# Two attention and GLU layers on one core: two weight pairs under way at a time, normalising and masking also on GpSimd, and another planned order

## The chip, the core and the metric

The kernel runs on one core of one Trainium2 chip. A core has five engines that run their own instruction streams side by side: TensorE (PE in the profile, its weight loads PEld) multiplies, VectorE (DVE) and ScalarE (ACT) work element by element and copy results out of PSUM, GpSimd (POOL) works element by element on SBUF alone, and SyncE (SP) issues most of the DMAs. Engines wait for each other through semaphores. The metric is the time of one execution on the device in microseconds (us). The time before is 389.96 us, the median of three runs (389.87 to 390.82).

## What is computed

A block A (sliding, dilated attention) and a block B (gated product) follow each other twice, each on the layer norm of x and each added to x. The sequence is 2048 rows of 448 columns; attention has 16 heads of 28 columns, and each row looks at itself and at 7 earlier rows, 2 apart. All is bfloat16.

```python
def _A_ref(x, wqkv, wo):
    q, k, v = qkv[0], qkv[1], qkv[2]            # x @ wqkv, 16 heads of 28
    idx = pos[:, None] - off[None, :]           # off = 0, 2, .., 14
    logits = jnp.einsum("bhsd,bhswd->bhsw", q, kg) * scale   # kg = k at idx
    logits = jnp.where(mask[None, None, :, :], logits, -1e9) # mask = idx >= 0
    attn = _softmax(logits, axis=-1)
    o = jnp.einsum("bhsw,bhswd->bhsd", attn, vg)
    return o @ wo

def _B_ref(x, w_gate, w_up, w_down):
    return ((x @ w_gate) * (x @ w_up)) @ w_down  # 448 -> 1792 -> 448

x = x + _A_ref(_layernorm(x), A_wqkv, A_wo)
x = x + _B_ref(_layernorm(x), B_w_gate, B_w_up, B_w_down)
x = x + _A_ref(_layernorm(x), A_wqkv, A_wo)
x = x + _B_ref(_layernorm(x), B_w_gate, B_w_up, B_w_down)
```

## The kernel before

x lies in SBUF as 16 blocks of 128 rows (x_sb). The four stages are numbered 0 (A), 1 (B), 2 (A), 3 (B); each is cut into chunks of rows, A0 and both B into 256, 512, 512, 512, 256 and A2 into four of 512. The list SEQ gives the chunks' rough sequence, so that work of a B chunk runs between the parts of an A chunk. The names below have the form name(stage, chunk or block or query block, ...), as the code's keys do.

**Layer norm and transposes.** ln_chunk makes the statistics of each block on DVE (bn, mv), the reciprocal deviation on ACT (lnv, rstd), and the normalised rows on DVE (xn, into one of five buffers xn_sb). For stage 0 PE transposes them (Tps, line 802; line 798 for the first two), and ACT or DVE copies them to xnTa (T). In the other stages the DMA engine transposes, issued by SP (line 791).

**Attention.** qk_chunk multiplies with WQK (line 535, key Kps/Qps), and ACT or DVE copies K and Q to qk (line 898). v_group makes V for a pair of query blocks. attn_front masks Q into two halves, Qz (line 1009: two instructions on DVE, one buffer for all groups), which zero the columns of the heads that are not meant; a burst of 64 small matmuls makes the scores S (line 1021), ACT takes the exponential (line 1030) and DVE applies the sliding mask (line 1037). attn_back makes another burst, AV (line 1055), copies the sums to O_sb, and norm divides. y_blocks multiplies with wo_g. The last heads' V (vt) is carried through DRAM: SP issues seven small DMAs a chunk (vt<-qk, line 907) and transposing loads (line 918).

**The B block.** b_chunk makes gate and up for each 128 of 1792 columns, two products side by side in the upper and lower 64 rows of PE (line 535); ACT copies the gate (g_sb, line 1146), DVE multiplies (hT, line 1149), and a second product with WD follows, added to x by DVE (line 1110).

**Bursts.** A burst's small matmuls use up instructions fast. Where a wide product is at hand, the planner puts some of its pairs into the burst as strips of 32 columns (line 538): 8 strips for a pair, 16 or 24 in a burst.

**Weights.** plain_dma (line 627) puts a DMA on SP's queue. WGU (gate and up) is loaded in two halves of columns of three pieces each (KPARTS), and every piece is a pair of DMAs, one for gate and one for up; WD follows in four pieces. The loop at line 726 makes each pair wait for the pair before it, through `gate`; the first pair waits for wo_g, and wo_g for x's third group of blocks (line 724). The pieces of one half share a semaphore, and a mode number tells the groups on it apart.

**What sets the order.** Nothing is ordered by hand. Each piece of work is handed to a planner (Sched) with the engines that may do it, an estimated duration for each, what it depends on, and a priority: the chunk's, plus PR for its kind, JP for its chunk and XP for single pieces. schedule runs a clock over these estimates; whenever an engine is free it takes the ready piece with the lowest number, and where two engines may do it, whichever comes first. HOLD_A, HOLD_BA and HOLD_BB say how long bursts may be held back to stand together, JOIN how many bursts may be joined, A_CAP and B_CAP how many PSUM banks each kind may hold. run_pe also estimates when a block of PE's instructions has been fetched, by fixed durations LINE_H, LINE_W and LINE_T for three phases of the run. emit then writes the instructions of each engine in this order, with semaphore waits: each engine runs them strictly in sequence, and so does SP's DMA queue.

## Time and profile before

| | |
|---|---|
| median of the runs | 389.96 us |
| profiled execution, its own time | 391.56 us |
| its span, first to last instruction | 389.6 us |
| PE busy | 380.8 us, 98% |
| DVE busy | 287.0 us, 74% |
| ACT busy | 209.0 us, 54% |
| POOL busy | 7.8 us, 2% |
| mean granted clock of TensorE | 0.996 |
| SP's and the other engines' plain DMAs (q1) | 54372 packets, 21.08 MB |
| instruction fetches (q8) | 52 packets, 0.85 MB |

The profiled execution is one execution, and the page and the trace tell of it alone. "Busy" of PE counts matmuls from their start to a modelled end, so that pipelined ones overlap. "issue" in the chain of work is time in which an engine waited for nothing that the profile shows. Line 535 is a helper that records every paired product, so one has to go by the tiles: xnTa,WQK is Q and K, WV,xnTa is V, wo_g,oT the attention's output, xnTb,WGU gate and up, WD,hT the second product of B.

### The profile page before, as it was taken

The page shows a single profiled execution, that of the slowest core. Times are in us where ns is not written, and L with a number is a line of the kernel's source. Part 1 is how long each engine was busy: PE and PEld are TensorE (multiplying, and loading weights), DVE is VectorE, ACT ScalarE, POOL GpSimd, SP SyncE. Part 2 cuts the span into 40 slices and gives each one's busy share as a digit, 9 for nine tenths or more (in the row PEclk, how much of TensorE's full clock was granted, in tenths as well). Part 3 has the DMA queues.
Part 4 walks back from the last instruction along what each step waited for, and adds up shares of the span by engine and source line. Part 5 has one row for each costly group of instructions (what it writes and reads, how often), then busy time and mean ns, then how long its engine had stood idle before and what let it go on. Part 6 is the DMA issues. An engine that isn't in the chain of part 4 may idle for free.

```text
span 389.6 us, 14816 instructions
## 1 busy us (share of the span) xinstructions
PE 380.8 (98%) x6565; PEld 214.7 (55%) x6565; DVE 287.0 (74%) x638; ACT 209.0 (54%) x393; POOL 7.8 (2%) x37
## 2 busy tenths in 40 slices
PE   8989989899999999999999999999999999999997
PEld 3646558455555544454766557654555444544584
DVE  6998989599968975399656997575967994376343
ACT  4887865397455775246454455565634842263140
POOL 6010000000000000000000000000000000000000
PEclk9989999999999999999999999999999999999999
DMA  8543574710711313004113132310133042100201
GB/s 276 161 106 76 137 101 124 122 23 9 87 25 34 47 39 56 10 6 86 21 22 50 30 63 37 75 32 2 27 54 96 3 47 52 48 2 3 60 14 49
DMA packets 54867, 22.53 MB, mean 58 GB/s; under 512 B 44996, under 2 KB 54804, under 8 KB 54804
## 3 DMA queue, kind: packets, MB, share of 16 engines
q1 hardware_dynamic: 54372, 21.08, 27.4%
q8 instruction: 52, 0.85, 0.9%
q10 hardware_dynamic: 432, 0.52, 0.5%
q14 instruction: 11, 0.09, 0.1%
HBM read 8.54 MB, written 2.71 MB: 29 GB/s over the span
## 4 chain that ended last, share of the span: by engine, by line
PE 93%; ACT 3%; DMA 1%; issue 1%; DVE 1%; SPq 0%; ACTq 0%
PE ps L535 82%; PE ps L538 3%; PE ps L1055 2%; PE ps L1021 2%; PE ps L697 2%; ACT E_sb L1030 1%; PE ps L1161 1%; DMA WD<-in_B_w_down_dram 1%; ACT xnTa L812 1%; ACT qk L898 1%; ACT g_sb L1146 0%; ACT xnTa L809 0%; DVE x_sb L1110 0%; PE ps L802 0%; DVE hT L1149 0%
## 5 line engine op out<-in xcount | busy, mean ns | idle before, releaser
L535 PE MATMUL ps<-xnTb,WGU 64*128 64x512 bf16 (+1 forms) x1908 | 174.4, 332 | 0.2
L535 PEld LDWEIGHTS ps<-xnTb,WGU 64*128 64x128 bf16 x1908 | 92.6, 94 | 67.8 <-issue 1.1
L1146 ACT ACTIVATE g_sb<-ps 128x512 bf16<-128x512 f32 (+1 forms) x140 | 71.1, 511 | 87.8 <-PE ps L535 71.7
L1149 DVE TENSOR_TENSOR hT<-g_sb,ps 128x512 bf16<-128x512 bf16 (+1 forms) x140 | 79.6, 576 | 43.1 <-ACT g_sb L1146 40.7
L535 PE MATMUL ps<-WD,hT 64*128 64x448 bf16 x778 | 78.6, 349 | 1.5 <-DMA WD<-in_B_w_down_dram 1.4
L535 PEld LDWEIGHTS ps<-WD,hT 64*128 64x128 bf16 x778 | 36.9, 94 | 36.0 <-issue 1.7
L535 PE MATMUL ps<-xnTa,WQK 64*128 64x512 bf16 (+1 forms) x492 | 55.2, 360 | 0.5 <-ACT E_sb L1030 0.3
L1110 DVE TENSOR_TENSOR x_sb<-x_sb,ps 128x448 bf16<-128x448 bf16 x62 | 36.4, 615 | 23.3 <-PE ps L535 23.3
L1030 ACT ACTIVATE E_sb<-ps,shift_sb 128x1024 bf16<-128x1024 f32 (+1 forms) x36 | 36.8, 1073 | 24.5 <-PE ps L1021 24.4
L767 DVE BATCH_NORM_STATS2 st<-x_sb 128x6 f32<-128x448 bf16 x64 | 37.7, 612 | 0.2
L788 DVE TENSOR_SCALAR xn_sb<-x_sb,mv,rstd 128x896 bf16<-128x896 bf16 (+1 forms) x64 | 34.7, 568 | 2.7 <-ACT rstd L772 2.5
L535 PEld LDWEIGHTS ps<-xnTa,WQK 64*128 64x128 bf16 x492 | 23.9, 96 | 22.2 <-issue 1.5
L898 ACT ACTIVATE qk<-ps 128x1024 bf16<-128x1024 f32 (+1 forms) x26 | 24.6, 956 | 11.3 <-PE ps L535 11.2
L535 PE MATMUL ps<-wo_g,oT 64*128 64x448 bf16 x256 | 29.1, 349 | 0.1
L1037 DVE TENSOR_TENSOR E_sb<-E_sb,MK 128x1024 bf16<-128x1024 bf16 (+1 forms) x36 | 23.6, 661 | 6.8 <-ACT E_sb L1030 6.5
L1081 ACT ACTIVATE R_sb<-R_sb 128x480 f32<-128x480 f32 (+1 forms) x34 | 20.5, 603 | 11.1 <-DVE R_sb L1080 10.6
L535 PE MATMUL ps<-WV,xnTa 64*128 64x336 bf16 (+3 forms) x248 | 23.1, 304 | 0.0
L1080 DVE STREAM_SHUFFLE R_sb<-O_sb 128x480 f32<-128x480 f32 (+1 forms) x34 | 23.1, 696 | 0.0
L1093 DVE TENSOR_TENSOR oT<-O_sb,R_sb 128x480 bf16<-128x480 f32 (+3 forms) x36 | 22.0, 624 | 0.8 <-ACT R_sb L1082 0.6
L1009 DVE TENSOR_SCALAR Qz<-qk,qmask 128x960 bf16<-128x960 bf16 (+1 forms) x36 | 14.7, 451 | 9.2 <-PE ps L1021 8.0
L1082 ACT ACTIVATE R_sb<-R_sb 128x480 f32<-128x480 f32 (+1 forms) x34 | 20.0, 600 | 0.3
L535 PEld LDWEIGHTS ps<-wo_g,oT 64*128 64x128 bf16 x256 | 12.4, 94 | 12.4 <-DVE oT L1093 0.9
(64 smaller groups left out, 231.6 us busy)
## 6 DMA issues: line engine op xcount, KB each, us to landing
out_dram<-x_sb SPq DMA_DIRECT2D x15, 112.0 KB, 1.7
x_sb<-in_A_x_dram SPq DMA_DIRECT2D x3, 448.0 KB, 6.0
WGU<-in_B_w_gate_dram SPq DMA_DIRECT2D x4, 224.0 KB, 3.6
WGU<-in_B_w_up_dram SPq DMA_DIRECT2D x4, 224.0 KB, 3.9
WD<-in_B_w_down_dram SPq DMA_DIRECT2D x2, 448.0 KB, 4.0
WGU<-in_B_w_gate_dram SPq DMA_DIRECT2D x2, 336.0 KB, 4.5
WGU<-in_B_w_up_dram SPq DMA_DIRECT2D x2, 336.0 KB, 6.3
vt<-qk SPq DMA_DIRECT2D x42, 16.0 KB
```

The source lines that it names most:

```text
L535: return lambda E: E.matmul(out(), lhs(), rhs(), start=start, stop=stop)
L767: sc.add("dve", one(lambda E, B=B: E.bn_stats(st6[:, B, :], x_sb[:, B, :]), ("bn", li, B)), 525.0, deps=[("x", li - 1, B)] + ([("xn", li - ...
L788: sc.add("dve", one(lambda E, B=B, dst=dst, src=src: E.tensor_scalar(dst, src, mv[:, B, 0:1], rstd[:, B:B + 1], ALU.subtract, ALU.mult), ( ...
L898: return E.activation(dst, src, ACT.Copy) if hasattr(E, "activation") else E.tensor_copy(dst, src)
L1030: return E.activation(E_sb[:, slot, 2 * hp:2 * hp + 2, 0:w], ps[:, b0:b0 + 2, 0:w], ACT.Exp, bias=shift_sb[:, 0:1], scale=SCALE)
L1037: return E.tensor_tensor(e, e, MK[:, kind, 0:nc].unsqueeze(1).unsqueeze(1).to_broadcast([128, 2, w // nc, nc]), ALU.min)
L1080: sc.add("dve", one(lambda E: E.stream_shuffle(R_sb[:, rs, 0:w], O_sb[:, os_, 0:w], [DH] * 32), ("Rs", li, qb)), dve_est(w) + 20.0, deps=[ ...
L1081: sc.add("act", one(lambda E: E.activation(R_sb[:, rs, 0:w], R_sb[:, rs, 0:w], ACT.Ln), ("Rl", li, qb)), act_est(w, False), deps=[("Rs", l ...
L1093: return E.tensor_tensor(oT[:, :, a % HALF:a % HALF + z - a], O[:, :, a - tok:z - tok], R_sb[:, rs, 0:w].rearrange("p (h n) -> p h n", h=4 ...
L1110: sc.add("dve", one(lambda E: E.tensor_tensor(x_sb[:, B, :], x_sb[:, B, :], ps[:, bk[w], 0:D], ALU.add), ("x", li, B)), dve_est(D), deps=[ ...
L1146: sc.add("act", one(lambda E, gs=gs, bk=bk: E.activation(g_sb[:, gs, 0:nt], ps[:, bk[0], 0:nt], ACT.Copy), ("G", li, j, fc)), act_est(nt), ...
L1149: sc.add("dve", one(lambda E, gs=gs, bk=bk, fc=fc: E.tensor_tensor(hT[:, fc, hs, 0:nt], g_sb[:, gs, 0:nt], ps[:, bk[1], 0:nt], ALU.mult), ...
```

## The change

Weights: the pieces of WGU, wo and WD now wait for the group two before, through a list `gates` of which each takes the last but one. The first pair waits for x's third group of blocks, the second for the fourth. wo_g is issued behind the first half of WGU and waits for that half's second pair; the second pair of the second half waits for wo_g together with the third pair of the first half; the ones for vt follow the first pair of the second half. Every piece has a semaphore of its own.

GpSimd: xn of stage 0 (but for the first chunk) and Qz of both A stages may be done by DVE or by GpSimd, whichever the planner finds free first. In the order that results, GpSimd does xn of blocks 2, 4, 8, 10, 14 and 15 and nine of the eighteen Qz.

Planner: the fixed durations of an instruction fetch give way to line_at, which takes into account the DMAs that were issued before and have not landed. JOIN, the HOLDs, ATT_P, B_CAP, HEAD_P, PR, JP and XP have other values. Together these give another order on every engine. The work is otherwise the same. The diff, without PR, JP and XP (lines of many numbers each):

```diff
-JOIN = 3
+JOIN = 2
-HEAD_P = (-7243.45, -6839.28, 6873.65, 2231.18, -2220.8)
-HOLD_A = 5940.0
-HOLD_BA = 13780.0
-HOLD_BB = 680.0
+HEAD_P = (-9131.1, -8282.44, 5502.77, 2529.68, -2872.96)
+HOLD_A = 4650.0
+HOLD_BA = 10410.0
+HOLD_BB = 1210.0
-ATT_P = 3.0
+ATT_P = 0.5
-B_CAP = 6
+B_CAP = 8
...
+    LINE_A = 1200.0
+    LINE_B = 1100.0
+    LINE_C = 2700.0
...
+    def line_at(self, at):
+        t = at + self.LINE_A
+        for issued, landed in self.moves:
+            if issued <= at + self.LINE_B:
+                t = max(t, landed - self.LINE_B)
+        return t + self.LINE_C
...
-            self.lines.append(at + (self.LINE_H if at < self.HEAD_T else self.LINE_W if at < self.HEAD_W else self.LINE_T))
+            self.lines.append(self.line_at(at))
...
-    plain_dma("sp", ones_dst, ones_src, ("vones",), "d_one", deps=["c_ones"] + [("wo", j) for j in range(4)], lat=4000.0, prio=-44.5)
-    for j in range(4):
-        dst = wo_g[32 * j:32 * j + DH, :, :]
-        src = A_wo.rearrange("(c j e) d -> j e c d", c=4, j=4, e=DH)[j]
-        plain_dma("sp", dst, src, ("wo", j), "d_wo", deps=["c_wo", ("x", -1, 11)], lat=3600.0, prio=-45)
-    gate = [("wo", j) for j in range(4)]
+    plain_dma("sp", ones_dst, ones_src, ("vones",), "d_one", deps=["c_ones", ("wu", 1, 0)], lat=6000.0, prio=-44)
+    gates = [[("x", -1, 11)], [("x", -1, 15)]]
     for n in range(2):
         f0, f1 = F // 2 * n, F // 2 * (n + 1)
         for i, (a, z) in enumerate(KPARTS):
             for w, lo, src in (("wg", 0, B_w_gate), ("wu", 64, B_w_up)):
-                plain_dma("sp", WGU[lo:lo + 64, a:z, f0:f1], src[64 * a:64 * z, f0:f1].rearrange("(k p) f -> p k f", p=64), (w, n, i), f"d_{w}{n}", deps=gate, lat=LOAD_L + 224 * (z - a) / RATE, prio=-44, mode=i)
-            gate = [("wg", n, i), ("wu", n, i)]
+                plain_dma("sp", WGU[lo:lo + 64, a:z, f0:f1], src[64 * a:64 * z, f0:f1].rearrange("(k p) f -> p k f", p=64), (w, n, i), f"d_{w}{n}{i}", deps=gates[-2], lat=1900.0 + 1000.0 * (z - a), prio=-44, est=650.0)
+            gates.append([("wg", n, i), ("wu", n, i)])
+        if n == 0:
+            for j in range(4):
+                dst = wo_g[32 * j:32 * j + DH, :, :]
+                src = A_wo.rearrange("(c j e) d -> j e c d", c=4, j=4, e=DH)[j]
+                plain_dma("sp", dst, src, ("wo", j), "d_wo", deps=["c_wo"] + gates[-2], lat=4000.0, prio=-44)
+            gates[-1] = gates[-1] + [("wo", j) for j in range(4)]
...
-        plain_dma("sp", WD[:, a:z, :], B_w_down[128 * a:128 * z, :].rearrange("(c p) e -> p c e", p=128), ("wd", n), f"d_wd{n // 2}", deps=gate, lat=LOAD_L + 112 * (z - a) / RATE, prio=-44, mode=n % 2)
-        gate = [("wd", n)]
+        plain_dma("sp", WD[:, a:z, :], B_w_down[128 * a:128 * z, :].rearrange("(c p) e -> p c e", p=128), ("wd", n), f"d_wd{n}", deps=gates[-2], lat=4200.0, prio=-44)
+        gates.append([("wd", n)])
...
-            sc.add("dve", one(lambda E, B=B, dst=dst, src=src: E.tensor_scalar(dst, src, mv[:, B, 0:1], rstd[:, B:B + 1], ALU.subtract, ALU.mult), ("xn", li, B)),
-                   325.0 if par == 0 else 540.0, deps=[("rstd", li, B), ("mv", li, B), ("x", li - 1, B), prev], prio=prio - 0.2)
+            sc.add(("dve", "pool") if li == 0 and j else "dve", one(lambda E, B=B, dst=dst, src=src: E.tensor_scalar(dst, src, mv[:, B, 0:1], rstd[:, B:B + 1], ALU.subtract, ALU.mult), ("xn", li, B)),
+                   {"dve": 325.0 if par == 0 else 540.0, "pool": 800.0}, deps=[("rstd", li, B), ("mv", li, B), ("x", li - 1, B), prev], prio=prio - 0.2)
...
-        sc.add("dve", [((lambda E, a=a: fz(E, a)), ("Qz", li, g) if a else None) for a in range(2)], 2 * (4 * (end - tok) * 0.33 + 62.0), deps=qdeps + [zprev, "c_qm"], prio=prio)
+        sc.add(("dve", "pool"), [((lambda E, a=a: fz(E, a)), ("Qz", li, g) if a else None) for a in range(2)], {"dve": 2 * (4 * (end - tok) * 0.33 + 62.0), "pool": 2 * (4 * (end - tok) * 1.25 + 100.0)}, deps=qdeps + [zprev, "c_qm"], prio=prio)
```

## The prediction

> **What bounds it.** I read the page first, then PE's busy time in stretches of 3.4 us, then the chain of work in the stretches that stood out, then the waits, the DMA queues and single rows for prices.
>
> ```profile
> PE 380.8 (98%) x6565; PEld 214.7 (55%) x6565; DVE 287.0 (74%) x638; ACT 209.0 (54%) x393; POOL 7.8 (2%) x37
> PEclk9989999999999999999999999999999999999999
> q8 instruction: 52, 0.85, 0.9%
> PE 93%; ACT 3%; DMA 1%; issue 1%; DVE 1%; SPq 0%; ACTq 0%
> ```
>
> PE is the bound: 93% of the chain. A new order can only take back the time in which PE stands or runs slowly, so I looked for that. The stretches (window, its length, busy of PE, PEld, DVE, ACT, POOL, granted clock, DMA share, GB/s):
>
> ```profile
> 19.81:23.22 3.41, 3.28 (x82) 1.54 (x74) 3.14 (x9) 2.95 (x10) 0.45 (x3) 1.00 0.19 47
> 23.22:26.64 3.42, 1.88 (x94) 1.41 (x96) 3.42 (x12) 3.42 (x6) 0.57 (x3) 1.00 0.34 96
> 26.64:30.05 3.41, 3.41 (x34) 2.11 (x30) 2.02 (x4) 2.30 (x4) 0.00 (x0) 0.50 0.83 186
> 47.12:50.53 3.41, 2.19 (x84) 1.29 (x82) 2.25 (x4) 3.17 (x6) 0.00 (x0) 1.00 0.59 88
> 67.60:71.01 3.41, 2.00 (x30) 1.32 (x30) 2.48 (x6) 1.83 (x6) 0.00 (x0) 1.00 0.88 217
> ```
>
> Four losses show. From 23.22 PE is busy 1.88 of 3.42 us while DVE and ACT are full (3.42 each): the layer norm and copies behind the transposes are late. The next stretch is granted half the clock (0.50), which costs 1.7 us. At 47 and 67 PE stands again. From 90 us on, PE is busy 10.00 of 10 us nearly everywhere. The chain, and the wait behind the last loss:
>
> ```profile
> 48.59 0.22 PE ps L1021 x16
> 48.81 1.22 issue
> 50.03 0.47 PE ps L1021 x26
> ...
> 66.43 3.96 DMA WD<-in_B_w_down_dram
> 70.48 1.50 PE ps L535 x14
> ```
>
> ```profile
> PE ps L535 <- DMA WD<-in_B_w_down_dram: 1.4, 1, 1.4
> ```
>
> At 66.43 the last quarter of WD is issued, four microseconds before PE needs it. At 48.81 PE waits in a burst of small matmuls for nothing that a semaphore tells. The DMA view of 44 to 47 us has only this for its queues:
>
> ```profile
> q1 hardware_dynamic: 471, 0.67, 95.1%
> ```
>
> In 47 to 50 one packet of the instruction queue appears. By the page that queue moved 52 packets, 0.85 MB, 16 KB each, for PE's 13,130 instructions (two a matmul): one block is 126 matmuls. I read the stand as a code block held behind the last weight pair, which filled the engines until 47.
>
> **The change, part by part.** The changed program has as many matmuls within 20 and the same products; its first 100 and last 25 of 391 PE groups follow nearly the old sequence.
>
> Weights. Before, one pair (gate and up piece) is under way at a time: issues at 16.4, 21.0, 25.7, 32.3, 37.1, 42.3, and WD from 52.1 to 66.4, landing at 70.4. Now the first pair waits for x block group 2 (11.5 us, where wo was issued) and two are under way; wo goes behind the first half of gate and up, 4 issues of about 0.4 us on SP. Bytes: 3.2 MB WGU, 1.6 MB WD, 0.4 MB wo. At the 224 GB/s of the 44 to 47 view they need 23 us, so the earliest end is 35 us; with nothing gained by the overlap it is 65. I take a cycle of 2.9 us a pair of two pieces (between 2.05 of data and 4.65 now), 4.0 for three: 19.6 + 2.5 for wo + 8 for WD, an end at about 42. First uses are at 55 (WGU) and 68 (WD), so WD's wait goes: 1.4. Next late is hT of the first B chunk, whose last row ends at 68.4, before the wait's start at 69.1; its chain has 0.4 us steps, so at most 0.6 of the gain is lost to it. I take -1.3, bounds -1.4 and -0.8.
>
> SP. Every weight issue now stands ahead of the first vt<-qk (before, six stood behind it). SP is past its last weight wait at about 38 by the same cycles; vt<-qk was issued at 38.92. If it were late, the vt loads are wanted at 80 (30 us of cover), the first xnTb transposes (47.6 before) at 55.6: 8 us of cover. The ones load now follows WGU's second half and is wanted only by those vt loads. Nothing.
>
> Head. Six of the sixteen xn and nine of the eighteen Qz go to GpSimd, and four more xnTa copies go from ACT to DVE. DVE's own work ahead of xn of the last-but-one block, summed by rows (statistics 0.612 + 0.170, xn 0.403, xnTa 0.416, Qz 0.345 or 0.464, casts 1.22, masks 0.45), is 25.8 us before (the trace has it at 25.9) and 20.4 after. So PE paces this stage. After 9.78 it has, up to its thirteenth narrow transpose, 28 pairs of 256 columns at 0.112, 28 of 512 at 0.216 (94.08 to 97.10 is 14 pairs), V 2.0 and 13 transposes at 0.2: 13.8 us, so 23.6; the copies that free the banks hold S(0,0) to about 24.6. What PE had done at 30.9 before is then done at about 28.4, with full clock between. I take -2.2. It cannot exceed the gaps (0.9 + 0.8 + 0.5 in the chain and waits) plus 1.7 for the clock, -3.9; if the gaps stay and a second stretch goes to half clock it is +1.7. With half the head's gain gone to lateness the clock still decides: the stretch from 23.22 would need to fall to 1.9 us again, while 47.12 at 2.19 and 67.60 at 2.00 kept the clock.
>
> GpSimd. No row shows tensor_scalar there. Its copies of 448 and 64 elements took 558 and 272 ns: at 0.745 ns an element xn (512) is 0.6 us and one Qz half (960) 0.94, or 1.2 in proportion to 558. A Qz pair is 1.9 to 2.4 us against 0.93 on DVE. There is one Qz buffer, so the pair must fit between two S bursts: written S(layer, last query block), the nearest are S(0,16) to S(2,0), with 4.5 us of gate and up pairs between, and S(2,4) to S(2,6), 7 us. Hidden. Side by side the engines cost each other a little: DVE's L705 copy took 279 ns alone and 309 to 327 beside GpSimd. 24 operations at 50 ns are 1.2 us of DVE, off the path; in the head 8 of them, 0.4 us, lie inside the bounds.
>
> The Trainium skill speaks against this part: "SBUF — State Buffer", Who interferes with whom, has a DVE operation in a two-port mode and a GpSimd operation hold one port pair exclusively, so the second waits for the whole first. By it the head's eight GpSimd operations would block DVE up to 0.6 to 1.2 us each, not 0.05; the sum by that rule is -0.3, the second rival's, against -2.5. The rows above show tens of nanoseconds, but no GpSimd operation there ran over 0.56 us.
>
> Code blocks. The 1.22 us stand at 48.81 loses its pair in flight: -1.2. But from 11.5 to 40 the engines are now filled nearly all the time. Between the call of the stalled block and its need PE ran 160 matmuls, 6.65 us by my count along the trace; in the new order 160 matmuls pass in 6.5 us from after S(0,0) to AV(0,2), and in 6.3 from AV(0,0) on. Each may stand from 0 to 4.2 (the 1.2 seen, plus 3 us of a second pair's 0.67 MB at 224 GB/s). I take 0.9 each, near the one stand that was seen: net +0.6, bounds -1.2 and +7.2. "Runtime: NRT & Kernel Launch", Instruction fetch mechanics, in the Trainium skill calls the cost of crossing a block mostly hidden; by that this term would be nothing and the sum 0.6 lower, against the 1.22 us row.
>
> Bursts. Small matmuls go with strips of a wide product. An S burst with 24 strips of WD stands at 118.63 for 1.00 us, 0.57 of it three wide pairs of 448 columns at 0.19; with 16 strips of gate and up at 202.07 for 0.97, 0.43 wide: 0.43 against 0.54 lost. Counting the new order, four S bursts go from 24 to 16 strips, one the other way, and one joined pair of AV bursts is split while another is joined: +0.4. JOIN, ATT_P, the HOLDs and caps act only through this order; triples were not used.
>
> Sum: -1.3 - 2.2 + 0.6 + 0.4 = -2.5. The profiled execution took 391.56 (span 389.61 and 1.95 around it), so 389.1 there; it lies 1.60 above the median of the runs, 389.96, so 387.5 on their scale.
>
> **Rivals.** Two pairs in flight starve PE of code: both tight places stand 3.2 rather than 0.9, +4.6, in all 392.1. It ends over 391.1 from a stand of 2.7 each on. For it: 48.81, with one pair in flight. Against: blocks in flight with pairs at 25 and 37 us cost no visible stand.
>
> GpSimd holds up DVE in the head: where DVE must let each of eight operations of 0.6 us end, 4.8 us of its 5.4 are gone, PE waits as before, the clock halves again, and the head's gain is 0, so 389.7. For it: DVE is full there and xn is in PE's path. Against: the L705 rows.
>
> All gaps of the head and the clock go (-3.9), and no block is late (-1.2): -1.4 - 3.9 - 1.2 + 0.4 = -6.1, 383.9. For it: DVE's sum falls 5.4 us. Against: PE's own 13.8.
>
> **How the numbers follow.** The forecast 0.46 (its own range 385.6 to 388.7), all gaps 0.16, GpSimd holds 0.15, starved code 0.23. I take 0.3%, 1.2 us, as what a measurement tells from no change. Faster 0.62, same 0.15, slower 0.23. The range 383.9 to 392.1 leaves out the outer halves of the two end cases, 0.08 and 0.11.
>
> **What would show it.** Right: PEclk full after the first 7 us; no wait on WD; WD's last issue by 40; xn and Qz rows of GpSimd near 0.6 and 1.0 us; S(0,0) at about 25 and the first gate and up product 2 to 3 us ahead of 55.6. Wrong: "issue" of over 2 us in the chain at 27 to 40 (starved code); DVE xn rows far over 0.40 beside GpSimd's, or another stretch of 0.50. A stand after 90 us, where I expect none, would make the whole forecast wrong.

## The result, and the profile after

The changed kernel takes 395.62 us (median of four, 394.57 to 396.67) against 390.39 for the kernel before on the same chip: 1.0127 of it, 95% interval 1.0086 to 1.0169. It is 5 us slower; I had forecast 2.5 us faster. The profiled execution took 395.95 us with a span of 394.2 us, against 389.6 before. Times further down are medians of all executions, but the ratios leave out four slow ones (one of before_two_pairs, one of price, two of three_then_two_qz).

From the page of the changed kernel, its busy times, the granted clock in 40 slices of 9.9 us, the instruction queue and the shares of the chain:

```profile
PE 382.8 (97%) x6547; PEld 213.5 (54%) x6547; DVE 283.8 (72%) x618; ACT 207.1 (53%) x387; POOL 65.8 (17%) x63
PEclk9998999999999999999999999999999999999999
q8 instruction: 51, 0.84, 0.8%
PE 86%; ACT 3%; DVE 3%; issue 1%; POOL 1%
```

PE had 93% of the chain and has 86% now. DVE was relieved by 3 us; GpSimd (POOL) went from 7.8 us to 65.8. The stretches in question (window, its length, busy of PE, PEld, DVE, ACT, POOL, granted clock, DMA share, GB/s):

```profile
17.00:20.40 3.40, 1.91 (x18) 0.80 (x14) 2.13 (x7) 2.45 (x6) 3.40 (x3) 1.00 0.48 113
23.80:27.20 3.40, 2.04 (x44) 0.86 (x40) 2.31 (x8) 2.05 (x2) 3.40 (x3) 1.00 0.74 147
27.20:30.60 3.40, 1.65 (x64) 1.05 (x66) 1.64 (x7) 1.58 (x3) 2.33 (x7) 0.95 0.71 177
30.60:34.00 3.40, 3.40 (x55) 1.74 (x57) 1.26 (x4) 2.13 (x4) 0.00 (x0) 0.55 1.06 245
```

Before, DVE and ACT were full in the worst stretch. Now neither is: in the first three stretches PE is busy 1.65 to 2.04 of 3.40 us, DVE and ACT have room, and GpSimd is full in two of them and busy 2.33 us in the third. Only the fourth is granted about half the clock (0.55). What GpSimd does, each shape apart (count, busy us, mean ns of one):

```profile
L1020 POOL TENSOR_SCALAR Qz<-qk,qmask 128x960 bf16<-128x960 bf16 x14 | 38.7, 2772 | 185.5 <-PE ps L1032 160.4 <-DVE xn_sb L799 25.2
L799 POOL TENSOR_SCALAR xn_sb<-x_sb,mv,rstd 128x512 bf16<-128x512 bf16 x6 | 12.6, 2100 | 3.5 <-ACT rstd L783 3.5
L1020 POOL TENSOR_SCALAR Qz<-qk,qmask 128x512 bf16<-128x512 bf16 x4 | 6.3, 1573 | 17.8 <-PE ps L1032 17.8
```

One xn takes 2100 ns, where I had 600, and half a Qz 2772, where I had 940 to 1200. In the chain of work between 10 and 45 us, and in the waits of the same stretch, xn is in PE's path:

```profile
22.18 0.10 issue
22.28 0.41 POOL xn_sb L799
22.69 1.64 issue
24.33 1.43 POOL xn_sb L799
25.76 0.68 issue
26.44 2.08 POOL xn_sb L799
```

```profile
PEld ps L813 <- POOL xn_sb L799: 7.8, 6, 2.3
PE ps L813 <- POOL xn_sb L799: 5.4, 5, 1.8
```

PE's narrow transposes (line 813) wait 5.4 us, at five places, for blocks that GpSimd normalises, and the first scores S(0,0) start at 29.5 us, not at 25. The weights did what was forecast: no wait on WD is left, and its last issue is at 38.2 us:

```profile
28.39 0.62 SPq L637 DMA_DIRECT2D WGU<-in_B_w_gate_dram  x1
29.06 0.62 SPq L637 DMA_DIRECT2D WGU<-in_B_w_up_dram  x1
30.29 8.29 SPq L637 DMA_DIRECT2D WD<-in_B_w_down_dram  x4
46.23 2.38 SPq L918 DMA_DIRECT2D vt<-qk  x7
```

### The profile page after: what moved, and what is told of

Its sections match the earlier page's. It is cut to its first block, busy times and chain, and to the rows that moved or that the text cites. A ratio compares the mean times of both kernels' runs of the same rounds, so it can differ in the third digit from the quotient of the medians.

```text
span 394.2 us, 14800 instructions
## 1 busy us (share of the span) xinstructions
PE 382.8 (97%) x6547; PEld 213.5 (54%) x6547; DVE 283.8 (72%) x618; ACT 207.1 (53%) x387; POOL 65.8 (17%) x63
## 3 DMA queue, kind: packets, MB, share of 16 engines
HBM read 8.54 MB, written 2.71 MB: 29 GB/s over the span
## 4 chain that ended last, share of the span: by engine, by line
PE 86%; ACT 3%; DVE 3%; issue 1%; POOL 1%
PE ps L544 77%; PE ps L547 3%; ACT E_sb L1041 2%; PE ps L1032 2%; PE ps L1066 2%; PE ps L1172 1%; POOL xn_sb L799 1%; ACT g_sb L1157 1%; DVE E_sb L1048 0%; DVE v_sb L1001 0%; DVE R_sb L1091 0%; DVE xn_sb L799 0%; DVE oT L1104 0%; DVE st L778 0%; DVE x_sb L1121 0%
## 5 line engine op out<-in xcount | busy, mean ns | idle before, releaser
L544 PEld LDWEIGHTS ps<-xnTb,WGU 64*128 64x128 bf16 x1896 | 91.1, 94 | 69.4 <-ACT g_sb L1157 2.4
L544 PE MATMUL ps<-WD,hT 64*128 64x448 bf16 x792 | 80.5, 349 | 0.1
L1020 POOL TENSOR_SCALAR Qz<-qk,qmask 128x960 bf16<-128x960 bf16 (+1 forms) x18 | 44.9, 2506 | 203.3 <-PE ps L1032 178.1
L544 PEld LDWEIGHTS ps<-WD,hT 64*128 64x128 bf16 x792 | 37.7, 94 | 35.1 <-PE ps L544 0.5
L544 PE MATMUL ps<-xnTa,WQK 64*128 64x512 bf16 (+1 forms) x496 | 56.1, 360 | 0.3 <-ACT E_sb L1041 0.2
L1121 DVE TENSOR_TENSOR x_sb<-x_sb,ps 128x448 bf16<-128x448 bf16 x62 | 35.9, 615 | 15.7 <-PE ps L544 15.5
L799 DVE TENSOR_SCALAR xn_sb<-x_sb,mv,rstd 128x896 bf16<-128x896 bf16 (+1 forms) x58 | 33.4, 600 | 2.8 <-ACT rstd L783 2.5
L909 ACT ACTIVATE qk<-ps 128x1024 bf16<-128x1024 f32 (+1 forms) x29 | 26.4, 919 | 13.5 <-PE ps L544 13.3
L1048 DVE TENSOR_TENSOR E_sb<-E_sb,MK 128x1024 bf16<-128x1024 bf16 (+1 forms) x36 | 24.6, 688 | 9.5 <-ACT E_sb L1041 9.3
L544 PE MATMUL ps<-wo_g,oT 64*128 64x448 bf16 x256 | 29.5, 349 | 0.1
L781 ACT ACTIVATE lnv<-mv,eps_sb 128x2 f32<-128x2 f32 (+1 forms) x33 | 9.4, 293 | 21.9 <-DVE mv L780 21.7
```

Of the source, the lines that this page charges most:

```text
L544: return lambda E: E.matmul(out(), lhs(), rhs(), start=start, stop=stop)
L799: sc.add(("dve", "pool") if li == 0 and j else "dve", one(lambda E, B=B, dst=dst, src=src: E.tensor_scalar(dst, src, mv[:, B, 0:1], rstd[: ...
L909: return E.activation(dst, src, ACT.Copy) if hasattr(E, "activation") else E.tensor_copy(dst, src)
L1020: return E.tensor_scalar(Qz[:, zs, a, :, 0:end - tok], qk[:, 1, :, tok:end], qmask[:, a:a + 1], None, ALU.mult)
L1048: return E.tensor_tensor(e, e, MK[:, kind, 0:nc].unsqueeze(1).unsqueeze(1).to_broadcast([128, 2, w // nc, nc]), ALU.min)
L1121: sc.add("dve", one(lambda E: E.tensor_tensor(x_sb[:, B, :], x_sb[:, B, :], ps[:, bk[w], 0:D], ALU.add), ("x", li, B)), dve_est(D), deps=[ ...
```

## The experiments

All experiments take the orders that the planner made and edit them afterwards, so that nothing else is planned anew. Their line numbers are shifted by the code put in. This table has, for each, the first scores, the first gate and up product and the first product with WD (us in the profile), the span, the median time and its ratio to the kernel before with the 95% interval.

| kernel | first scores | gate, up | WD | span | time | ratio |
|---|---|---|---|---|---|---|
| before | 22.5 | 55.6 | 70.5 | 389.6 | 390.17 to 390.39 | 1 |
| changed | 29.5 | 60.7 | 73.2 | 394.2 | 395.62 | 1.0127 (1.0086 to 1.0169) |
| xn_dve | 24.6 | 54.3 | 66.9 | 388.4 | 390.09 | 0.9989 (0.9965 to 1.0013) |
| qz_dve | 28.6 | 59.4 | 71.8 | 392.5 | 394.36 | 1.0116 (1.0093 to 1.0139) |
| both_dve | 25.2 | 55.3 | 67.8 | 389.4 | 391.09 | 1.0024 (1.0006 to 1.0042) |
| before_two_pairs | 22.6 | 55.4 | 68.8 | 387.9 | 388.81 | 0.9950 (0.9925 to 0.9974) |
| before_xn_pool | 25.1 | 59.2 | 73.7 | 393.0 | 394.99 | 1.0103 (1.0053 to 1.0153) |
| price | 21.8 | 54.1 | 69.2 | 389.6 | 391.11 | 1.0012 (0.9975 to 1.0050) |
| one_then_two | 21.8 | 57.9 | 73.6 | 392.7 | 394.95 | 1.0118 (1.0074 to 1.0162) |
| tidy | 22.0 | 58.2 | 73.3 | 392.4 | 395.42 | 1.0117 (1.0074 to 1.0159) |
| three_then_two | 21.8 | 54.2 | 67.6 | 386.7 | 390.94 | 1.0036 (1.0004 to 1.0068) |
| three_then_two_qz | 22.1 | 55.4 | 68.8 | 387.9 | 393.58 | 1.0040 (1.0006 to 1.0075) |

The columns of the profile are those of one execution each, and the head of a kernel varies between executions: up to 80 us price is the kernel before, and its first scores come 0.7 us earlier and its first product with WD 1.3 us earlier. What follows the first product with WD varies less: it takes 319.1 to 319.3 us in the seven other kernels with the old order.

### The GpSimd operations back on DVE: xn_dve, qz_dve, both_dve

Three kernels: the changed one, with the six xn, the nine Qz pairs, or both put into DVE's order where the planner's clock had them.

```diff
+def to_dve(sc, kinds):
+    for got, seq in [u for u in sc.order["pool"]]:
+        op = got[0]
+        if op.ins[-1][1] is not None and op.ins[-1][1][0] in kinds:
+            sc.order["pool"].remove((got, seq))
+            op.eng = "dve"
+            at = next(n for n, (o, _) in enumerate(sc.order["dve"]) if o[0].start > op.start)
+            sc.order["dve"].insert(at, (got, seq))
...
     sc.schedule()
+    to_dve(sc, ("xn",))        # or ("Qz",), or ("xn", "Qz")
```

> The changed kernel with every order held, but the six xn that GpSimd did are put into DVE's order at the time that the planner gave them; the nine Qz stay on GpSimd. Theory (price): the change is slow because xn on GpSimd takes 2.1 us, not 0.6, and PE's narrow transposes in the first 30 us wait for it. Then the waits of PE for xn there (5.4 us) shrink to under 2, and the time falls by 4 to 5 us, to about 391. Rival (order): the new order itself is the slow part, so PE stands in the head whichever engine normalises, and the time stays at 394 to 396. Rival (ports): GpSimd and DVE hold each other up all along, also through Qz; then only about a third of the loss goes, 394.

> The changed kernel with every order held, but the nine Qz pairs of GpSimd are put into DVE's order; the six xn stay on GpSimd. Theory (price): a Qz pair of 5.35 us on GpSimd is hidden between bursts and costs the others nothing, so the time stays within 1.2 us of the changed kernel's 395.6. Rival (ports): DVE loses time beside GpSimd's 45 us of Qz, so that the time falls by 1.5 to 3 us. Rival (DVE full): nine pairs of 0.93 us come back to DVE at places where it is in the chain, and the time grows by 1 to 3.

> The changed kernel with every order held and all of GpSimd's xn and Qz put into DVE's order: what is left of the change is the weights and the new order. Theory (price): as with xn alone on DVE, about 391, within 1 us of that kernel. Rival (order): 394 to 396, as the change. Rival (ports): 1.5 us or more under the kernel with only xn on DVE.

Moving six instructions back takes the whole loss against the kernel before away, though not the miss against the forecast of 387.5: the time falls from 395.62 to 390.09, the span by 5.8 us, and PE's waits for xn shrink from 5.4 to 0.2 us. The stretches of xn_dve, columns as above:

```profile
17.00:20.40 3.40, 3.40 (x50) 1.86 (x47) 3.40 (x12) 2.85 (x10) 1.04 (x1) 1.00 0.43 106
23.80:27.20 3.40, 3.19 (x80) 1.93 (x82) 2.71 (x8) 3.06 (x6) 0.39 (x3) 1.00 0.81 160
27.20:30.60 3.40, 3.23 (x122) 1.69 (x119) 2.90 (x8) 3.32 (x4) 0.00 (x0) 1.00 0.64 167
```

PE is busy 3.19 and 3.23 us where it had 2.04 and 1.65. DVE, full from 17.0 to 20.4 us (3.40 of 3.40), carries the six xn with waits of 0.2 us at most, the clock is not halved any more, and the scores start at 24.6 us. Of the rivals, "order" falls as the cause of the 5 us, since nothing but the engine of six instructions changed.

Behind the head the Qz pairs are hidden: PE of xn_dve is 1.05 us ahead of both_dve at 80 us, and at every hundredth matmul from there to the end this lead stays the same to 0.02 us. In the head they are not quite. With xn on GpSimd, moving them changes 1.0127 to 1.0116, inside both intervals, but the first scores of qz_dve come 0.9 us earlier (28.6 against 29.5): in the changed kernel GpSimd makes the first Qz pair from 15.5 to 18.6 us, and an xn stands behind it. With xn on DVE, leaving them on GpSimd is 1.0 us better (388.4 against 389.4 of span, 390.09 against 391.09 of time): 0.6 of that is there when PE is at 21 us, where Qz(0,0) would stand in DVE's way. I had expected the two kernels within 1 us, which they just are.

The rival of the ports falls too as the cause of the 5 us. Behind it stands the rule of the Trainium skill, "SBUF — State Buffer", Who interferes with whom, by which, of a DVE instruction in a two-port mode and a GpSimd instruction, the second waits for the whole first. In the changed kernel's trace, rows of DVE that lie wholly beside a GpSimd xn or Qz against rows of the same shape that touch none: statistics 0.607 against 0.615 us (8 rows), xn 0.469 against 0.407 (6), the mask of 1024 elements, with two inputs in SBUF, 0.782 against 0.687 (10). Over 57.7 us of GpSimd work all such rows lost 1.1 us. One of the long ones (DVE's timeline, then GpSimd's):

```profile
13.55 0.78 DVE L799 TENSOR_SCALAR xn_sb<-x_sb,mv,rstd 128x512 bf16<-128x512 bf16 x1
```

```profile
13.43 2.07 POOL L799 TENSOR_SCALAR xn_sb<-x_sb,mv,rstd 128x512 bf16<-128x512 bf16 x1 [0.96 <-ACT rstd L783]
```

That xn took 0.78 us and not 0.40, so something is shared, but it did not wait the 2.0 us that were left of GpSimd's operation. Beside another form of GpSimd's it does wait so long; the kernel price, below, has two such rows.

### xn on GpSimd in the kernel before: before_xn_pool

The mirror of the first experiment: old weights, old order, and the same six blocks moved to GpSimd.

```diff
...
     sc.schedule()
+    to_pool(sc, (2, 4, 8, 10, 14, 15))    # xn of these blocks, from DVE's order into GpSimd's
```

> The kernel before with its orders held, but xn of blocks 2, 4, 8, 10, 14 and 15 done by GpSimd at the time the planner had for DVE. Theory (price): 2.07 to 2.18 us each on GpSimd, against 0.40 on DVE; PE's narrow transposes wait for them, and the time grows by 3 to 7 us, to 393 to 397. Rival (the new order made GpSimd late): in the old order the copies are wanted later and the time stays within 1.2 of before. Rival (ports): DVE's rows beside GpSimd grow by over 0.1 us each.

```profile
L799 POOL TENSOR_SCALAR xn_sb<-x_sb,mv,rstd 128x512 bf16<-128x512 bf16 x6 | 12.7, 2123 | 6.6 <-ACT rstd L783 5.9 <-PE ps L813 0.7
```

```profile
PE ps L813 <- POOL xn_sb L799: 5.4, 5, 2.2
```

Groups by shape, then waits of PE. The same 2.1 us and the same 5.4 us of waits, and 394.99 us. The price alone makes a kernel slow whose order is untouched. The rival of the ports fails here: the two xn of DVE that lie wholly beside one of GpSimd's took 0.39 us, no more than alone (0.41).

### What GpSimd asks for each form: price

The kernel before, with 48 operations on GpSimd from 80 us on, where it is idle; nothing reads what they write. The diff, in short:

```diff
+    ts1: E.tensor_scalar(buf[:, 0:n], W[:, 0, 0:n], sc32[:, 0:1], None, ALU.mult)
+    ts2: E.tensor_scalar(buf[:, 0:n], W[:, 0, 0:n], sc32[:, 0:1], sc32[:, 1:2], ALU.subtract, ALU.mult)
+    cp:  E.tensor_copy(buf[:, 0:n], W[:, 0, 0:n])
+    tt:  E.tensor_tensor(buf[:, 0:n], W[:, 0, 0:n], W[:, 1, 0:n], ALU.mult)
...
+    for n in (256, 512, 704):
+        for form in (cp, ts1, ts2, tt):
+            fns += 4 * [form(n)]
```

> The kernel before, and 48 extra operations on GpSimd behind its own work, from about 95 us on, on a scratch buffer that nothing reads: a copy, a product with one scalar, a difference and product with two scalars, and a product of two tensors, each four times with 256, 512 and 704 bfloat16 elements from the gate weights. Theory: the price goes by the number of arithmetic steps, not by elements alone: at 512 elements about 0.6 us for the copy, 1.56 for one scalar, 2.07 for two scalars, and the tensor product unknown, between 1 and 2.5; the time of the kernel stays within 1.2 us of before, and DVE's rows beside them within 0.05 us. Rival (ports): DVE's rows of two inputs or of copies grow by 0.3 us or more beside them, and the time by over 2. Rival (elements): all forms cost alike, about 0.75 ns an element, and the long xn was its buffers' doing.

GpSimd's groups by shape, of 512 elements:

```profile
L569 POOL TENSOR_SCALAR price_sb<-WGU,price_sc 128x512 bf16<-128x512 bf16 x4 | 8.3, 2072 | 0.4
L567 POOL TENSOR_SCALAR price_sb<-WGU,price_sc 128x512 bf16<-128x512 bf16 x4 | 6.2, 1562 | 0.4
...
L573 POOL TENSOR_TENSOR price_sb<-WGU 128x512 bf16<-128x512 bf16 x4 | 4.6, 1155 | 0.3
...
L571 POOL COPY price_sb<-WGU 128x512 bf16<-128x512 bf16 x4 | 2.4, 612 | 0.2
```

A copy is 0.61 us, a product of two tensors 1.16, a product with one scalar 1.56, a difference and a product with two scalars 2.07. The undisturbed rows of 256 and 704 elements (0.40 and 0.83 for the copy, 0.92 and 2.04 for one scalar, 1.22 and 2.71 for two, 0.67 and 1.52 for the tensors) give slopes of 0.97, 2.5, 3.3 and 1.9 ns an element: by form, not by elements. It is not the number of arithmetic steps alone either, as I had expected: the product of two tensors and the product with one scalar are one step each. xn in the changed kernel is the two-scalar form to within 2%, so its buffers had no part in it.

The time, 1.0012 (0.9975 to 1.0050), does not tell price from the kernel before, but the trace does. Matmul by matmul, PE is 1.30 us ahead of the kernel before at 119 us, and at 157 us only 0.19: it lost 1.1 us while GpSimd worked on 704 elements, where the other kernels with the old order lose nothing. PE's waits from 119 to 150 us, of which the kernel before has none:

```profile
PE ps L535 <- DVE x_sb L1132: 0.4, 1, 0.4
PE ps L535 <- DVE hT L1171: 0.2, 1, 0.2
```

Seven of DVE's rows beside GpSimd's extra work grew by 0.37 to 1.33 us. The worst are two halves of a Qz, beside GpSimd's products of two tensors (DVE's timeline, then GpSimd's):

```profile
144.92 2.73 DVE L1031 TENSOR_SCALAR Qz<-qk,qmask 128x512 bf16<-128x512 bf16 x2 [0.57 <-ACT qk L920]
142.79 6.31 POOL L573 TENSOR_TENSOR price_sb<-WGU 128x704 bf16<-128x704 bf16 x4
```

The two took 1.14 and 1.67 us, where one alone takes 0.34. Each ended about 0.15 us behind the end of an operation of GpSimd's (at 145.92 and 147.51), so here DVE did wait for GpSimd's operation to end. My 0.05 us was wrong, and the rival of the ports was right on DVE's rows (0.3 us or more), though not on the time (over 2 us). In all, DVE's rows that touched GpSimd's 65 us of extra work lost 4.6 us.

### Only the weights: before_two_pairs

Old order, the change's weights: all weight issues moved ahead of the first vt<-qk in SP's list.

```diff
...
     sc.schedule()
+    two_pairs(sc)    # gates of the change: each group waits for the group two before; wo behind the first half
```

> The kernel before with the order of PE, ACT, DVE and GpSimd held, and only the weights as in the change: two groups under way, wo behind the first half, all weight issues ahead of the first vt<-qk. My step for the weights: WD's wait of 1.4 us goes and so does the stand of 1.2 us at 48.81, while no other block of code is late: 387.5 to 388.7. Rival (starved code): new stands of 1 to 3 us in the bursts between 27 and 40 us, 390 or more. Rival (hidden anyway): hT or the layer norm of the B chunks is late next, and the time stays within 0.6 of before.

It is the one kernel that is faster than before, 0.9950 (0.9925 to 0.9974). In the profile the first product with WD is at 68.8, not 70.5, and the stand at 48.81 is gone; a new one has come (PE's waits between 10 and 120 us, then the instruction queue between 23.5 and 25.4 us):

```profile
PE ps L1049 <- issue: 1.0, 1, 1.0
```

```profile
q1 hardware_dynamic: 130, 0.20, 48.1%
q8 instruction: 1, 0.02, 4.4%
```

This is what my starved-code rival meant, at one place and not two: a stand of 1.04 us at 25.60. The trace's packets of the instruction queue bear the reading out. In the kernel before, that block moves from 22.00 to 22.94 and nothing stands; with two pairs it moves from 23.95 to 25.29, and PE goes on at 26.63, 1.3 us after. Before, the block of the 48.81 stand moved from 47.24 to 48.50, and PE went on 1.5 us after; with two pairs it moves from 44.93 to 46.35, and nothing stands.

That the two pairs took the stand at 48.81 away is not shown, though. In price, with the old weights, that block moved from 43.84 to 45.11, and nothing stands at this matmul either; in before_xn_pool, also with the old weights, 0.5 us do. price has a stand at another place instead, at 42.34 (its waits from 10 to 60 us):

```profile
PE ps L1077 <- issue: 0.4, 1, 0.4
```

The wait on WD, in contrast, is there in all three traces with the old weights (1.4, 1.6 and 1.1 us) and in none with two pairs under way.

### Other gates for the weights: one_then_two, tidy, three_then_two, three_then_two_qz

If two pairs in flight hold the block back, one pair until 27 us should free it. The diff, in short, with notes behind #:

```diff
+    # one_then_two: wo first, as before; (0,1) and (0,2) wait for the pair before, the rest for the group two before
+    back = 1 if (n, i) in ((0, 1), (0, 2)) else 2
+    # tidy: also the small WQK copies of DVE on GpSimd, and ACT's first exponential behind the next two xnTa copies
```

> The kernel before with its compute order held and the weights in a third way: wo and the first three pairs one after the other as before, two groups under way from there on, every weight issue ahead of the first vt<-qk. Theory (a code block is held behind two pairs): the new stand of 1.0 us that two pairs brought at 25.6 goes, the stand at 48.8 stays away, WD's wait too: 387.0 to 388.0, 0.7 to 1.5 under the kernel with two pairs from the start. Rival (the block is late whatever the weights do): a stand of about 1 us remains between 24 and 30 us, and the time stays at 388.8.

> As the kernel with one pair and then two, and two small edits in the head: the three small WQK copies of DVE go to GpSimd (0.22 to 0.27 us each there), and ACT's first exponential goes behind the two xnTa copies that follow it. Theory (the half clock follows from PE's gaps): PE's gaps at 23 to 25 shrink by 0.5 to 0.8 us, the busy time of that stretch rises above 2, the clock stays at 1.0, and with the 1.7 us of the half clock the time is 385.0 to 386.5. Rival (the clock halves whatever the gaps): only 0.3 to 0.8 us come off. Rival (another copy is late next): nothing comes off.

The stand at 25.6 went as expected: PE is 1.7 us ahead of before_two_pairs at 42 us (0.8 of that already at 11 us, ahead of any stand). Then it is lost and more: 394.95 us, 1.0118 (1.0074 to 1.0162). PE's longest wait, and SP's queue:

```profile
PE ps L535 <- DMA xnTb<-xn_sb: 4.4, 1, 4.4
```

```profile
37.22 7.05 SPq L653 DMA_DIRECT2D WD<-in_B_w_down_dram  x4
44.37 2.61 SPq L932 DMA_DIRECT2D vt<-qk  x7
49.62 2.47 SPq L943 DMA_TRANSPOSE v_sb<-vt  x2
52.14 1.30 SPq L816 DMA_TRANSPOSE xnTb<-xn_sb  x1
```

and the same queue in before_two_pairs:

```profile
29.82 8.70 SPq L656 DMA_DIRECT2D WD<-in_B_w_down_dram  x4
39.53 3.42 SPq L935 DMA_DIRECT2D vt<-qk  x7
44.64 3.37 SPq L946 DMA_TRANSPOSE v_sb<-vt  x2
48.20 1.26 SPq L819 DMA_TRANSPOSE xnTb<-xn_sb  x1
```

SP works in order. WD's four issues, each held by its gate, end at 44.3, the first vt<-qk behind them goes at 44.4 instead of 39.5, and the xnTb transposes, two steps further back in the queue, come 3.9 us later, when PE wants them. Both of my theories missed this: the block was freed, and the queue took back more than that gave. In tidy the clock was halved all the same, and the exponential that I moved became a wait of its own:

```profile
PE ps L1059 <- ACT E_sb L1068: 1.7, 1, 1.7
```

It ends where one_then_two does, 1.0117 (1.0074 to 1.0159). tidy therefore does not tell what the half clock costs.

So the next kernel takes WD's issues out of the way of vt<-qk, and gates the pairs of the first half one by one from 11 us on:

```diff
+    back = 1 if n == 0 or i == 0 else 2
...
+    # WD's four issues behind the first seven vt<-qk; in three_then_two_qz also Qz(0,0) on GpSimd
+    sc.order["sp"] = sp[:at] + one(first) + sp[at:vt] + one(last) + sp[vt:]
```

> The kernel before with its compute order held and the weights a fourth way: the first pair at x's third group as in the change, the pairs of the first half and the first of the second one after the other, two groups under way from there on, and WD's four issues behind the first seven vt<-qk on SP instead of ahead of them. Theory (a code block is held behind two pairs, and SP's queue passes a late end of the weights on to the xnTb transposes): no stand near 25, none near 48, none at WD, and the first gate and up product at about 53 again, not 58: 386.7 to 387.7. Rival (the transposes were late for another reason): a stand of 3 us or more remains before the first gate and up product, 391 or more. Rival (the code block is late elsewhere): a new stand of 1 us or more between 28 and 50, 388 or more.

> The same, with the first Qz pair (512 columns) alone on GpSimd, at 1.56 us each. Theory (hidden Qz): its scores stand 5 us behind it in PE's order, DVE has 0.6 us less to do at 16 us, where xn waits, and PE's gaps at 22 to 25 shrink by 0 to 0.6: 0 to 0.6 us faster than without it. Rival: S(0,0) waits for GpSimd, 1 us or more slower.

The profile has what I expected, a span of 386.7 and the first gate and up product at 54.2, but not without stands (PE's waits between 10 and 120 us):

```profile
PE ps L535 <- ACT O_sb L1096: 1.2, 1, 1.2
PE ps L1085 <- issue: 0.9, 1, 0.9
```

A block is late at 40.8 us, so the rival "late elsewhere" has its due; price and tidy have a stand of 0.4 us in the same burst. And the timed runs don't follow the profile: their median is 390.94 us, but they spread from 388.6 to 394.4, 1.0036 (1.0004 to 1.0068) together, half of them with the clock granted in full and at or under 390.3, half with one to three half-clock stretches and 391.6 or more. The profile shows one of the first half only. In the kernel with Qz(0,0) on GpSimd (1.0040, 1.0006 to 1.0075, with the same spread) the load of xnTb is waited for by 1.5 us, so a wait on the edge may be what tips; that is argued, not shown. The two kernels are not told apart, and the step of Qz(0,0) stays open.

## Why the prediction was wrong, point by point

**The step that failed** is the price of GpSimd in the head: "at 0.745 ns an element xn (512) is 0.6 us". It was taken from copies. A copy does cost that (0.61 us), but xn is a difference and a product with two scalars, and costs 2.07 to 2.18. I wrote that no row showed tensor_scalar there, and then bounded it by scaling rows of copies; the upper end, 1.2, was for Qz and still a copy's. Six times 1.5 us more are 9 us of GpSimd, and PE waited for 5.4 of them.

This step explains 5.5 of the 8.1 us between the forecast and the measured time (387.5 and 395.62): without it, as xn_dve, the kernel takes 390.09, as long as before, and not 387.5. The other 2.6 us lie in what the new order gives and costs (Head, Code blocks, and Bursts and order below). By the spans of single executions the parts are: weights -1.7 (389.6 to 387.9), order and Qz +0.5 (to 388.4), xn on GpSimd +5.8 (to 394.2). By the median times, which the profiled executions of before and before_two_pairs exceed by 1.0 us or more, they are -1.4 (390.24 to 388.81), +1.3 (to 390.09) and +5.5 (to 395.62).

The mechanism was none of my three rivals. "GpSimd holds up DVE" had the right engine and the wrong victim: not DVE, but the transposes behind xn itself. "Starved code" had the right sign, for another reason: no stand of that kind shows in the changed kernel.

**Head, -2.2.** With xn on DVE it holds: I had S(0,0) at 24.6 and the clock full, and xn_dve has 24.6 and 1.00. Against before_two_pairs it is 1.9 us ahead at the first WD product (66.9 against 68.8). But GpSimd's relief of DVE, on which I had founded the gain, made at most half of it. With nothing moved to GpSimd, both_dve still has the full clock and is 1.0 us ahead (67.8 against 68.8). DVE begins the last-but-one xn at 23.2 us there, against 25.5 before, with 20.1 us of work ahead of it instead of 21.4: the new order puts half of the early Qz, a mask and a cast behind it. So the size was right in part by luck.

The clock's 1.7 us is nearly right where it arises, but did not reach the end. With the same order and other weights, PE of three_then_two, at the full clock, and of price, at half the clock from 25.2 to 28.6, are level at 25 us, and at 31 us three_then_two is 1.5 us ahead; at the first gate and up product they are level again (54.2 and 54.1), after two waits of 0.9 and 1.2 us in three_then_two. Of 69 timed executions of the kernel before, 26 had a mean granted clock of 0.998 or more, and their median is 390.21 us; 38 had 0.994 to 0.997, about one half-clock stretch of 3.4 us, and theirs is 390.15. So one such stretch does not show in the time of the kernel before. The five others, at 0.991 or less (two such stretches or more), took 394.05 to 394.67. What takes the one stretch's cost up in the kernel before is not shown.

**Weights, -1.3.** Right: the wait on WD (1.4 us) went, and nothing stood in its place; before_two_pairs is 1.4 us faster by the medians.

**SP, nothing.** Right for the change (the vt<-qk went at 46.2, behind late Q and K, not behind weights), but the cover was wrong. I counted 30 us for vt and 8 us for xnTb each by itself. They are links of one queue: vt<-qk, v_sb<-vt, xnTb. With the last weight issued at 38.2 (before_two_pairs) the transposes were in time, with 43.9 (one_then_two) PE stood 4.4 us.

**Qz hidden.** Right behind the head, though a pair takes 5.35 us and not 1.9 to 2.4. In the head, right with xn on DVE; beside xn on GpSimd the pair held an xn up.

**Code blocks, +0.6.** Mis-sized. In the old order a stand of 1.0 us came at 25.6. In the changed kernel none shows, where PE waits for GpSimd; but in xn_dve, where it does not, no "issue" of PE is longer than 0.2 us from 10 to 120 us either. So the two stands of 0.9 us that I counted did not come. The 1.2 us at 48.81, which I let the change win back, are there in one execution of the old weights and not in another.

**Bursts and order, +0.4.** Mis-sized. From the first WD product to the end xn_dve takes 321.5 us and before_two_pairs 319.1: the new order costs 2.4 us there and gives the head's gain back. It is the order and not the execution: the four profiles with the new order have 320.7 to 321.6, seven of the old one 319.1 to 319.3. One piece can be named, PE's wait in a burst that carries strips of the next gate and up product:

```profile
PE ps L1044 <- DMA xnTb<-xn_sb: 0.8, 1, 0.8
```

From 70 to 385 us PE is not busy for 1.6 us in xn_dve and for 0.3 in before_two_pairs. That is 1.3 us, the 0.8 among them; the other 1.1 us lie in time in which PE counts as busy. That these are in the bursts, of which more have 16 strips now, is argued, and no run tests it.

## What to carry to other kernels

A price is good for one form on one engine: before work moves to an engine that has never done it, look for a row of the same operation with the same operands, and where there is none, let the upper bound be several times the nearest row, above all where the result is on the path of the bound engine. An engine with room that is five times slower makes a good home for work with slack (Qz) and a bad one for work in a chain (xn), even if the engine relieved is full. In a queue that runs in order, the cover of a transfer is that of the tightest one behind it. And a stand that one execution shows, as the one at 48.81, is worth a look in a second one before a change is credited with it.

## What the runs showed of the hardware that I had not expected

- GpSimd at 512 bfloat16 elements: copy 0.61 us, tensor product 1.16, one scalar 1.56, two scalars 2.07. DVE did the last two in 0.34 and 0.40. The Trainium skill, "GPSIMD Engine Reference", Engine selection, has it about two times slower with two inputs and near line rate with one; for these forms with a scalar the runs say 4.6 and 5.2 times.
- On GpSimd a product of two tensors is cheaper than one with a scalar (slopes 1.9 and 2.5 ns an element). But beside GpSimd's products of two tensors DVE's Qz took 1.14 and 1.67 us instead of 0.34, and ended only after them; beside GpSimd's xn the longest xn of DVE took 0.78 instead of 0.41.
- After a code block has moved, PE goes on 1.3 to 1.5 us later in the six stands (0.4 to 1.2 us, in six traces) where both times can be read.
- A half-clock stretch of 3.4 us put PE back by 1.5 us in price against three_then_two, and left the median of the kernel before unchanged (390.15 and 390.21).
